# A Nystrom attention and expert-layer kernel whose order of work is laid down anew

## The chip, the cores and the metric

The kernel runs on one core of one Trainium2 chip. The metric is the time of one execution on the device in microseconds (us), as the median of several runs. One more execution was profiled; its trace gives the instructions of every engine: TensorE (PE, its weight loads PEld), VectorE (DVE), ScalarE (ACT), GpSimd (POOL), and SyncE (SP), which issues nearly all DMAs.

## The reference, cut to what matters

```python
# q, k, v: 8 batches, 8 heads, 576 rows, 64 columns; 32 landmarks (means of 18 rows)
A  = sm(q, k_lm);  Bm = sm(q_lm, k_lm);  C = sm(q_lm, k)     # sm: softmax of scale * a @ b.T
Z = Bm.T / (norm1(Bm) * norminf(Bm) + 1e-6)
for _ in range(6):
    Z = 2 * Z - Z @ Bm @ Z
x = A @ Z @ C @ v                  # then reshaped to 4608 tokens of 512
logits = normed(x) @ normed(expert_emb).T / tau              # 8 experts
expert_idx = argmax(logits); gate_w = softmax(logits)[expert_idx]
out[token] = gate_w * (relu(x @ w1[expert_idx]) @ w2[expert_idx])   # w1 512x1024, w2 1024x512
```

## The kernel before, in words

The kernel works batch by batch, and the steps of the eight batches are woven into one another. For a batch b it guesses the one expert that all its tokens choose, loads that expert's weights, and checks the guess at the end (a general path follows when a guess fails).

Steps of a batch, each a Python generator in `nystrom_moe` (L477): `loads` (L638, keys and queries, 1152 KB each; those of batch 0 in two parts), `load_values` (L655, two halves of 640 KB, two buffers), `sums` (L666, the landmarks' means, on POOL and DVE or DVE alone), `guess` and `choose` (L1150, L1171, the expert), `inverse` (L691) and `powers` (L1020, the six steps of the inverse; batches 2 and 3, 4 and 5, 6 and 7 are taken together), `values` (L798, pooled-query scores), `weighted` (L872, the landmarks' values), `queries` (L914, attention scores) with `scored` (L941, their softmax, with `both`, L977, a subtraction or a product on POOL or DVE), `landmarks` (L1069), `rows` (L1192, router scores and norms of the tokens, two steps a batch), `weights` (L1318, four loads of 512 KB for w1 and four for w2), `first_scale` (L1339, each quarter of w1 squared and summed at L1348), `first_weights` (L1369, the landmark products folded into w1), `scaled` (L1401, their split into two 16-bit parts), `second_weights` (L1426, the scale and the split of w2), `first` (L1487, the first layer: six products of 288 columns a chunk), `second` (L1516, the second layer: three products of 512 columns a chunk) and `outputs` (L1556, scaling on ACT or DVE, and the store). All products except transposes and warming are issued through the helper at L514.

Some buffers tie the steps: eight PSUM banks; of these four in a row ("quad") are used by one step at a time among `values`, `queries`, `rows` and `first_weights`; two buffers for keys, queries and values; four each for the quarters of w1 and of w2.

The order of all this is written out by hand in four constants: TURNS (L59), a string of 2614 two-character numbers, each of which names the generator that goes on next; CHOICES, which engine a step takes where there is a choice; BANKS, which PSUM banks a step gets; and WARM, at which turn how many units of 128 columns of warming products are put ahead of a step. `Weave.run` (L222) walks through them, and each engine's instructions, and SP's DMAs, are issued in the order of the walk:

```python
        for turn, n in enumerate(turns):
            ask, got = self.asks[n], None
            if ask[0] == "any":
                option = ask[1][int(next(choices))]
...
            elif ask[1] == "pe":
                if turn in WARM:
                    warm(WARM[turn])
...
                    got = self._banks(int(next(banks)), ask[6])
            self._step(n, got)
```

`keep_warm` (L600) issues the warming products, whose results nobody reads, into the last bank (L604), up to 512 columns each. They stand only in the first part of the program, before the first layer of batch 0.

Of the kernel before, what the change touches and what calls it, by code (L numbers as in the profile page):

```python
# [59 lines left out]
    "0606063306330033000706060700340c0b340b38013801010001010800383e000100083f010h013636013g3g003j3k360c37010101010c"  # L60
    "01360h0136390c0139003j0i013j1i013u3k3u013w3u3x3v3x1j3w3x1j3w3w3x3v1i3x3n3x3u3x3x3k3h3x3x3l3x3x1k3l3x3u3v3x3x3h"
    "3u1m3h1k3u3x3h1i0d3x3x3h3w1k3h3a3u3v3a1i1i1j021k3w0d3a1l411i021k3u02413u410e1l3w1k1k1k1k3u3w3w1k1i3a1k02001k1k"
    "1i0e1l411k3w1k1k3a020n1k1k3u1k413o1k421k1k1k3w1k1j1k3u3m4602421k46421k3m1l1k0n3a2m1j1j1j3w1j3a432m462m49431m49"
    "2m02022m4h3a3m2m2m3m024i3m4h1n3o023w3o3a2m1m02024k4l0i4j4j4m1m4i4m021m2m2m2m4o3a022m2m1m4p4o024p1n2m1n1n1n4q2m"
    "023a1n4r4q1m1m2n4u1n0i021m1m1m1m024p1m2m1m022m0i4u1m2m0o4t4s4v1n4t2m2m4x4z1m4s4x2m1m504z510o4v1m51524w4w2n2m2m"
    "1m4p1o2n1m1m55502n2m1m524w2n3b542n1m1p541o1o1o4r1m2n3b1m4y2n564y1m1m4w3b4w4y563b3p4w3p584w59551p1r0o4y2n2n2n59"
    "2n53584w2n2n4w534w3c583c0o533c3c2n2n4w2n2n1r4r532n592n4w2n3c2n2n1p0t1o4q5c2n1o2n4w3c1o1r4n4n5c585c584w1o591r3d"
    "5c4w033d584w2n2n2n2n591p032n593d035h0j2n4n5h5h4n585h4w4w2n1p2n4n03581p4n031r2n1p58035h5h5h0358035h5h5h5h5b3q03"
    "1r034a2n03591r5b2n1r3q1r035b2n0303033q3q2n033q2n581r1p2n5j03031p3q5g2n5d035k0359595k5l5l5d5k5j5g5k1q2n4b1p5k58"
    "5l581p5n5m3q5l0j592n5m2n592n2n2n1r1r2n595l3q1r5n1r5m595l5n2n1r2n4b5q4b5l2o372o1r2o5d2o5r5l3q5l5p5l5s5s5s5s5s5p"  # L70
    "1r5u5s5u5s3q5l0k5g3q3q5l2o5w1r2o5z5l5w5x5z2o2o2o5w2p5x5l5v5l0k5x5y5v1r2o2o5y1r2o5t5t1r63612p5l0u5t2p2o5t605l1r"
    "605t0p645l64632p611r2o5t4d4d3r4d0u1r663m664d3q3r4d2p3a4d3r5j0t683r2p682o6868683r6g2o4d4d3s6h6g676h6h6h3s3s0z3s"
    "3s2o673t2o5p4d3t3t0p1s1s4d6j6i1t1t2o2o1s2p674c6i1s4c6o6m6j1s6m2p2o6n6o1t366n1t2o6p6p6a2o6q2o6o2p1s6a6r1s6r6q6n"
    "6a6k1t2p2p2p2p2p6n6s0q6k2p1t6t6u6o2p1u6k2p6n6k6o6n6u6n6u2p1u6u0q6n1s4d1w2p0z1t1u6k2p6u2p6u2p6u0u7a6n6n6n0u6k7a"
    "6o6k6n6o6k4d792p7a6k6o6o796o6n1t6k6k2p2p2p2p2p2p2p791u6o7c7c4e2p6o6o7c2p6v4e1u1w6w6v6w1u1w6v4e102p4e2p2p6v2p6v"
    "6v6c6c104f7b6c6c781w6c781w7b2p6c4f4f7f1w1u1u2p691u782p7b2p4f7f1u7f4f1w7f0v2p1w4f152p1w1u1w4a7e7g7f7g7g1v7h6c71"
    "2p1w1w2p1w6c7h7j7e7i2p2p2p7h0v2p3n4g2p7i2p0w4g7i706b6b7n4g7l1w7o7j0w1w1w7l7j107m107l7m2q2q2q2q7j7r1w1y2q7n2q2q"
    "1w1w1w2q7u1x1x7o2q2q1w7v7t7s2q7t1y2q2q1x1x1x1x7o7x7r2q7o7x7e2q2q7z2r7v2q7s807z7w2q2q1y1y7y1x7w7o1z7y2q1w7q8015"
    "7n6c7u7q7n1x1w6c2q1w2q6c2r2r2r1y827q1y1y812q2q6c2r847n81828e7m848d2r2r8c8e7o8d7q1z2r8c2r7n2r717n2r7o717o8i218h"
    "048j2r2r8j041z8j1z7o161z7n7j2r042r211y21041z047o042r2r212r2r8j1z7o047m8j7m8j7m1z7m8g7n8g16048g2r042104047m7m6c"  # L80
    "212r2r2r1z1z8j2r8p2r2r212r2r217m21218q2r2r8o041b1z8p7n04047m7m2r8r8q202r047n048o1b047m8s0404218t8o048p7n914d8s"
# [34 lines left out]
WARM = {20: 36, 39: 6, 42: 2, 51: 13, 63: 19, 77: 4, 86: 10, 93: 21, 104: 24, 123: 19, 157: 9, 188: 19}  # L116
# [1571 lines left out]
```

## Time and profile before

| what | us |
|---|---|
| median of 3 runs | 401.57 (401.19 to 401.67) |
| the profiled execution | 400.33 |
| its span, first to last instruction | 398.6 |
| TensorE busy | 382.6 |
| DVE busy | 319.3 |
| ACT busy | 252.8 |
| POOL busy | 88.0 |

The profiled execution's own time stands beside its span: 1.7 us lie around the span. A profile's "idle before" of an instruction is time in which its engine did nothing, and the name behind the arrow is what ended it; "issue" means that nothing shown there was waited for. The mean granted clock of TensorE over the span is 0.999 of full speed.

### The profile page before, as it was taken

To read this page: it belongs to the slowest core of one execution; us is meant where nothing else is said; L and a number is where in the kernel's file an instruction comes from. 1 tells how busy PE (TensorE), PEld (TensorE's weight loads), DVE (VectorE), ACT (ScalarE), POOL (GpSimd) and SP (SyncE) were. 2 spreads that over 40 slices of the span, in tenths; PEclk is the share of its full clock that TensorE was granted. 3 is DMA by queue.
4 is the path that set the end of the run, shared out by engine and by line. 5 is a ranking of instruction groups with operands and counts; after the bars stand their busy time and mean duration, and the time that the engine had idled before them with its cause. 6 is when DMAs were issued, how large, how long until landed. Compare 5 with 4: busy or idle time off the path is not lost.

```text
span 398.6 us, 15203 instructions
## 1 busy us (share of the span) xinstructions
PE 382.6 (96%) x6390; PEld 237.4 (60%) x6390; DVE 319.3 (80%) x916; ACT 252.8 (63%) x627; POOL 88.0 (22%) x91
## 2 busy tenths in 40 slices
PE   3999999999999999999999999999999999999994
PEld 1456755586645775567754675557745675467644
DVE  5899998899898999977989999747896798747431
ACT  1369969578589779735978678155659749445310
POOL 4154255211203132302335711101101201000100
PEclk9999999999999999999999999999999999999999
DMA  8887973563695996226786776114480266116012
GB/s 305 344 323 321 389 268 124 154 248 118 181 407 212 303 404 226 74 71 236 242 322 244 249 224 216 63 42 152 133 314 12 81 196 242 53 47 233 2 41 88
DMA packets 22669, 78.78 MB, mean 198 GB/s; under 512 B 2752, under 2 KB 5056, under 8 KB 20800
## 3 DMA queue, kind: packets, MB, share of 16 engines
q1 hardware_dynamic: 22304, 77.54, 53.7%
q8 instruction: 52, 0.85, 0.9%
q10 hardware_dynamic: 288, 0.18, 0.2%
q14 instruction: 25, 0.20, 0.2%
HBM read 62.96 MB, written 14.75 MB: 195 GB/s over the span
## 4 chain that ended last, share of the span: by engine, by line
PE 85%; DVE 6%; ACT 5%; issue 1%; DMA 1%; POOL 0%; ACTq 0%; DVEq 0%
PE ps L514 82%; PE ps L604 3%; ACT junk L1232 2%; ACT ec L861 2%; DMA k_t<-kT 1%; DVE ww L1418 1%; DVE w2c L1472 1%; DVE cm L824 1%; DVE ht L1482 1%; ACT ht L1480 0%; DVE cneg L851 0%; POOL half L682 0%; ACT ww L1416 0%; PE ps L1105 0%; ACT w2c L1470 0%
## 5 line engine op out<-in xcount | busy, mean ns | idle before, releaser
L514 PE MATMUL ps<-w2c,ht 128*128 128x512 f16 (+2 forms) x1176 | 197.6, 340 | 0.1
L514 PEld LDWEIGHTS <-ht 128*128 128x128 f16 (+1 forms) x1176 | 94.7, 102 | 80.3 <-issue 1.4
L514 PE MATMUL ps<-ab,ww 128*128 128x288 f16 x768 | 100.7, 286 | 0.8 <-DVE gpr L1167 0.5
L514 PEld LDWEIGHTS <-ww 128*128 128x128 f16 x768 | 73.6, 98 | 23.9 <-issue 2.0
L1480 ACT ACTIVATE ht<-ps 128x288 f16<-128x288 f32 x128 | 47.5, 424 | 26.4 <-PE ps L514 24.8
L1482 DVE SCALAR_TENSOR_TENSOR ht<-ps,ht 128x288 f16<-128x288 f32 x128 | 53.8, 448 | 9.6 <-ACT ht L1480 8.7
L1232 ACT ACTIVATE junk<-ps 128x512 bf16<-128x512 f32 (+1 forms) x40 | 23.8, 596 | 26.2 <-DVE lga L1223 12.3
L1472 DVE SCALAR_TENSOR_TENSOR w2c<-wstage,wsc,w2c 128x1024 f16<-128x1024 f32 x28 | 37.4, 1337 | 3.0 <-ACT w2c L1470 2.8
L1348 ACT ACTIVATE junk<-wstage 128x1024 bf16<-128x1024 f32 x32 | 34.0, 1064 | 6.2 <-DMA wstage<-w 6.0
L1574 ACT ACTIVATE yt<-ps,gfac 128x512 f32<-128x512 f32 (+1 forms) x30 | 18.8, 627 | 22.7 <-PE ps L514 20.7
L861 ACT ACTIVATE ec<-ps,cneg 128x144 f32<-128x144 f32 x64 | 23.4, 390 | 11.0 <-DVE cneg L851 5.6
L1250 POOL TENSOR_TENSOR nrm<-ssq,half 128x5 f32<-128x5 f32 x8 | 10.4, 1300 | 85.6 <-ACT junk L1232 85.6
L981 POOL TENSOR_TENSOR ae<-ae,asum 128x576 f32<-128x576 f32 x11 | 12.7, 1157 | 71.3 <-DVE asum L795 23.3
L1432 ACT ACTIVATE junk<-wstage 128x1024 bf16<-128x1024 f32 x26 | 27.4, 1055 | 1.5 <-DMA wstage<-w 1.3
L1470 ACT ACTIVATE w2c<-wstage,wsc 128x1024 f16<-128x1024 f32 x21 | 24.2, 1159 | 2.8 <-DVE wsc L1443 2.8
L682 POOL TENSOR_TENSOR half<-q_t 128x576 f32<-128x576 f32 x13 | 19.5, 1500 | 28.8 <-DVE ht L1482 11.8
L972 POOL TENSOR_TENSOR ab<-at,ab 128x576 f16<-128x576 f32 x11 | 14.1, 1286 | 48.7 <-ACT ab L970 38.4
L1416 ACT ACTIVATE ww<-ps,wsc 128x1024 f16<-128x1024 f32 (+1 forms) x18 | 17.8, 1023 | 10.4 <-PE ps L514 9.1
L1418 DVE SCALAR_TENSOR_TENSOR ww<-ps,wsc,ww 128x1024 f16<-128x1024 f32 (+1 forms) x18 | 20.7, 1159 | 3.6 <-ACT ww L1416 3.6
L682 POOL TENSOR_TENSOR half<-k_t 128x576 f32<-128x576 f32 x11 | 14.5, 1314 | 21.5 <-DMA k_t<-kT 12.9
L981 POOL TENSOR_TENSOR ae<-ae,am 128x576 f32<-128x576 f32 x11 | 12.7, 1158 | 26.6 <-DVE am L955 25.0
L514 PE MATMUL ps<-wstage,wt 64*32 64x256 f32 x512 | 16.8, 380 | 1.0 <-issue 0.7
(220 smaller groups left out, 505.9 us busy)
## 6 DMA issues: line engine op xcount, KB each, us to landing
wstage<-w SPq DMA_DIRECT2D x64, 512.0 KB, 6.7
v<-v SPq DMA_DIRECT2D x16, 640.0 KB, 5.9
k_t<-kT SPq DMA_DIRECT2D x7, 1152.0 KB, 10.9
q_t<-qT SPq DMA_DIRECT2D x7, 1152.0 KB, 7.2
out<-yt SPq DMA_DIRECT2D x31, 256.0 KB, 2.9
abs__140<-ab SPq DMA_DIRECT2D x8, 576.0 KB, 3.8
k_t<-kT SPq DMA_DIRECT2D x2, 576.0 KB, 4.8
q_t<-qT SPq DMA_DIRECT2D x2, 576.0 KB, 6.7
```

The lines of the kernel that those rows point to most:

```text
L514: pe.matmul(o, lhsT, rhs, start=start, stop=stop)
L682: pool.tensor_tensor(out=half, in0=sv[:, :, :, 0:9], in1=sv[:, :, :, 9:18], op=ALU.add)
L861: act.activation(ects[g][:, QS * x:QS * x + QS], pc[:, a, c], AF.Exp, bias=neg[:, 4 * g + 2 * a + c:4 * g + 2 * a + c + 1], scale=SCALE / ...
L981: pool.tensor_tensor(out=x, in0=x, in1=z, op=op)
L1232: act.activation(junk[lo:hi, 0:512].rearrange("p (j g x) -> p j g x", j=4, g=2), pfv[lo:hi, :, n, :, 0:D], AF.Square, scale=1.0 / ASCALE, ...
L1348: act.activation(junk, stage[1, b, q], AF.Square, accum_out=sq[:, q:q + 1])
L1418: vec.scalar_tensor_tensor(out=ww[:, 1], in0=pw, scalar=sc, in1=ww[:, 0], op0=ALU.mult, op1=ALU.subtract)
L1432: act.activation(junk, stage[2, b, q], AF.Abs, accum_out=sq[:, q:q + 1])
L1470: act.activation(w[:, 0], st, AF.Copy, scale=sc)
L1472: vec.scalar_tensor_tensor(out=w[:, 1], in0=st, scalar=sc, in1=w[:, 0], op0=ALU.mult, op1=ALU.subtract)
L1480: act.activation(ht[:, 0, r], ph[:, 0:HS], AF.Relu)
L1482: vec.scalar_tensor_tensor(out=ht[:, 1, r], in0=ph[:, 0:HS], scalar=0.0, in1=ht[:, 0, r], op0=ALU.max, op1=ALU.subtract)
```

## The change

Only the four constants change. The generators, the instructions they issue, the shapes and the loads are the same. The strings say nothing to a reader, so here is the head of each, and WARM in full:

```diff
 TURNS = (
-    "0606063306330033000706060700340c0b340b38013801010001010800383e000100083f010h013636013g3g003j3k360c37010101010c"
+    "0606063333060b0b0007000033060607083c3c010836013601003600010001340c3f010c003g010c3h01013435013h340c010101340134"
...
 CHOICES = (
-    "01110001100100010000000000000000000100011111010000100000001000110010111100001011001010000000000010010000000000"
+    "01110011000100100000000000000000000100011001010000000000000100100011000011111001100010000000000000100010000000"
...
 BANKS = (
-    "40261016010541230201010107123012703436512370612020162063426325473420340130210456730113421242321413241232703170"
+    "00201616010531230201201107123701273453602371601771604701320341257302040120305467212031423141231423412134014021"
...
-WARM = {20: 36, 39: 6, 42: 2, 51: 13, 63: 19, 77: 4, 86: 10, 93: 21, 104: 24, 123: 19, 157: 9, 188: 19}
+WARM = {19: 36, 31: 5, 49: 13, 78: 16, 87: 15, 103: 21, 117: 21, 142: 12, 157: 9, 188: 7}
```

Walked through turn by turn, the two orders differ in this:

- **Loads at the start (SP).** Before: keys and queries of batch 0, values of batch 0, keys and queries of batch 1, then w2's first quarter, w1's first two, the first half of batch 1's values, w1's third and fourth quarter, the second half of the values, the rest of w2, the keys of batch 2. After: the same to the queries of batch 1, then w1's first two quarters, w2's first, w1's third, both halves of the values, w1's fourth, two quarters of w2, the keys of batch 2, and w2's last quarter.
- **The inverse of batch 0.** After, its first power is issued between the two halves of the attention scores of batch 0, where it came behind both; on DVE some transposes and reductions of the scores stand between the powers that stood ahead of them.
- **`weighted` of batch 4.** Before, `inverse` (4, 5), `first_weights` 3, the first power and `weighted` 4 follow one another; after, three chunks of the second layer (nine products of 512 columns) stand ahead of the first power.
- **The four banks in a row.** Between the two `rows` steps of batch 5: before, two chunks of the second layer and one power; after, five chunks, one chunk of the first layer and two powers. Between the second `rows` step of batch 3 and `queries` of batch 4: after, three chunks of the second layer and one power. Between the two `rows` steps of batch 1: the same chunks in both.
- **Choices.** Output scalings: 30 on ACT and 11 on DVE before, 24 and 17 after. `both`: 22 on POOL and 10 on DVE before, 27 and 5 after. Passes over w2 on DVE where ACT could do them: 13 before, 16 after.
- **Warming.** 182 units of 128 columns before, 155 after; before the first power and before the second half of `queries` 0 none is left.
- **The last stores** stand in the same order.

## Rows read from the trace of the kernel before

**Rows 1.** The page, head and part 1: share of the span.

```profile
span 398.6 us, 15203 instructions
PE 382.6 (96%) x6390; PEld 237.4 (60%) x6390; DVE 319.3 (80%) x916; ACT 252.8 (63%) x627; POOL 88.0 (22%) x91
```

**Rows 2.** The page, part 4: chain that ended last, by line.

```profile
PE ps L514 82%; PE ps L604 3%; ACT junk L1232 2%; ACT ec L861 2%; DMA k_t<-kT 1%; DVE ww L1418 1%; DVE w2c L1472 1%; DVE cm L824 1%; DVE ht L1482 1%; ACT ht L1480 0%; DVE cneg L851 0%; POOL half L682 0%; ACT ww L1416 0%; PE ps L1105 0%; ACT w2c L1470 0%
```

**Rows 3.** Windows: us, PE, PEld, DVE, ACT, POOL busy, clock, DMA share, GB/s.

```profile
0.00:40.30 40.30, 31.45 (x715) 17.92 (x716) 33.14 (x118) 20.29 (x51) 16.80 (x36) 1.00 0.84 322
40.30:393.60 353.30, 351.15 (x5676) 219.48 (x5675) 286.17 (x799) 232.02 (x576) 71.17 (x56) 1.00 0.52 185
393.60:398.60 5.00, 0.02 (x1) 0.00 (x0) 0.00 (x0) 0.47 (x1) 0.00 (x0) 0.96 0.16 51
```

**Rows 4.** Windows within the first 40 us, same columns.

```profile
18.50:26.55 8.05, 8.05 (x219) 4.44 (x204) 8.05 (x21) 3.34 (x6) 4.80 (x4) 1.00 0.83 295
26.55:35.10 8.55, 7.19 (x167) 4.04 (x164) 7.33 (x41) 7.21 (x15) 3.93 (x4) 1.00 1.02 398
35.10:40.30 5.20, 5.11 (x141) 3.80 (x141) 5.17 (x19) 5.20 (x13) 2.12 (x2) 1.00 0.55 211
```

**Rows 5.** Windows for L604 (warming) alone: us, PE, PEld; the sum.

```profile
18.50:26.55 8.05, 4.46 (x19) 1.63 (x20) 1.00 0.83 295
...
sum 28.60, PE 13.78 PEld 4.43; mean PE 3.44 PEld 1.11
```

**Rows 6.** Waits of PE, 40.3 to 394 us: total, times, longest.

```profile
PE ps L514 <- ACT junk L1232: 0.9, 3, 0.4
PE ps L514 <- issue: 0.6, 1, 0.6
```

**Rows 7.** Timeline of PE around 168.9: start, us, what, idle before.

```profile
167.76 0.52 PE L514 MATMUL ps<-v,ct 128*32 128x64 f32 x22
168.91 0.88 PE L514 MATMUL ps<-v,ct 128*32 128x64 f32 x48 [0.64 <-issue]
```

**Rows 8.** DMA queues, 166 to 167.6 us: packets, MB, share.

```profile
q1 hardware_dynamic: 36, 0.07, 12.2%
q8 instruction: 1, 0.02, 5.6%
```

**Rows 9.** DMA queues, 27.8 to 29 us.

```profile
q1 hardware_dynamic: 113, 0.42, 95.5%
q8 instruction: 1, 0.02, 4.9%
```

**Rows 10.** Timeline of PE, first-layer weights of batch 0.

```profile
30.24 0.40 PE L514 MATMUL ps<-wstage,wt 64*32 64x256 f32 x1 [0.68 <-issue]
```

**Rows 11.** Timeline of PE around the rows steps of batch 5.

```profile
263.56 0.57 PE L514 MATMUL ps<-wgd,ab 32*128 32x72 f16 x48
264.06 1.47 PE L514 MATMUL ps<-w2c,ht 128*128 128x512 f16 x6
265.46 0.65 PE L514 MATMUL ps<-ek 32*32 32x64 f32 x32
266.46 0.77 PE L514 MATMUL ps<-wgd,ab 32*128 32x72 f16 x72 [0.36 <-ACT junk L1232]
```

**Rows 12.** Timeline of PE, second rows step of batch 1.

```profile
100.20 0.77 PE L514 MATMUL ps<-wgd,ab 32*128 32x72 f16 x72 [0.41 <-ACT junk L1232]
```

**Rows 13.** Groups by line: output scaling on DVE.

```profile
L1572 DVE TENSOR_SCALAR yt<-ps,gfac 128x512 f32<-128x512 f32 (+1 forms) x11 | 7.8, 715 | 3.9 <-PE ps L514 3.8
```

**Rows 14.** DMA issues, 23.5-24, 24-24.5 and 25.8-26.2: KB, us to landing.

```profile
wstage<-w SPq DMA_DIRECT2D x1, 512.0 KB, 4.7
...
wstage<-w SPq DMA_DIRECT2D x1, 512.0 KB, 6.8
...
v<-v SPq DMA_DIRECT2D x1, 640.0 KB, 6.6
```

**Rows 15.** Timeline of PE: first expert product.

```profile
35.10 0.28 PE L514 MATMUL ps<-ab,ww 128*128 128x288 f16 x1 [0.49 <-DVE gpr L1167]
```

More of the change, by code (lines that the diff above doesn't have):

```diff
@@ L65 @@
[L65 to L69, printed above, removed]
@@ new lines @@
+    "3p3o3n3o3i3n1k1k3i3n3m1m3p3i3o3i3o38380d0e3m3p0e381k0202421k023p421i00421k2n383p3n3n1k1k021k3n1k1l1k1k021k1l1k"
+    "1k421k443s02381j3p1l1k1k023n1i3q1k1k001k1k471k1k0n3p3n3p1k3q1k421j44471j1k441l381k2m3p451j2m38471j493p452m3q1m"
+    "02022m4a3q492m2m022m3q4b0i3s4a4c4d0i3s1j2m024f4b1m2m4c4e1m384g2m2m1m2m4g4i022m0i0n4l4m1m024i02024e022m1m1m1m02"
+    "021m4k2m4e2m024l2n1m4j1m1n2m2m4x4w1m4u1m4y4k2m4w1m1m4x2m4j4w1m1n4u4y2m1m2m2m2m1m1n1m4e3838521n0i1n1m2n4z4v0o50"
+    "1n0o504z1o4v2n2n551o1m51511m522n381m391m1m534w54394w392n2n394w0t1o4w551r1m1p3t533t1o55582n542n2n584m591o2n2n2n"
@@ new lines @@
+    "4w55590o3a0o1r4w4w562n2n2n2n564w2n3a564l3a563a2n1o4m2n2n5b3a3a582n3b2n1r5b4w2n3b1o583b5b2n354w4h4h4w595d5b1n1p"
+    "035d1o1p4w4n4w4h4w5858031r5d031r2n2n1r2n2n5d4h58035d031n032n2n4h03032n0j591p5d584h592n4w3u1r5d5d0j0303035d034o"
+    "031p03591p033u5d3u2n5d5a591p3u035a582n3u590k033u5c2n5k58031r5859035k5k1p1r5g5k5c032n5k1p0k592n5a2n5g591p1p5n58"
+    "2n5l591q5o5n5l3u2n2n5p5o1r1r5n1r1r2n2n5l5p593u2n2n585o1r5p1r2n2n2n5l4o5q4o2p5l1r5l5r5l5l2o5s5t1r5g5q5l2o5v2o5w"
+    "5t2o5t5t5t5l5t5t5l5x5l2o2o5x5y1r3u343u5x2o2o2o1r5w2o602o0t612o0u601r0u3u635v625y5y1r5l5u5u5l5l5z6b3u5l3u5z5l1r"
@@ new lines @@
+    "635u625u2p6c1r5l0p5u2o2p5c615u6b2o1r6e4q2p4q3v6e4q3v4q4q4q3v3v3v2p6f2p6c6f2o6f6f6f4q0p644q2o653w6i6i5q6g6g3w2o"
+    "2o3w6i6i2o3w2o2p3w4q4q1t6k3x4p6j6c3x6k6j1t4p3x1t4q6n6o0u6m6l6n1t2o6p1t0q1s6o6o6m386n2o6n1w2o2p1s0u1t6q6l1s1s0z"
+    "656m652o6p2p6q6w6t1w6w6s6m6u2p2p1t6u2p1s2p6n2p2p2p6o6u6u6u6u6o6m6o6u6z6n0z6o6o6o6o2p2p1s2p1u6o1t4q2p6z6m6n6y2p"
+    "6m2p782p153q6m0q6m6y1s6m6n6z6n2p6r1s6m2p2p6y2p2p6x2p2p6x2p2p6n6m7a2p6n6m104r6v1u7a1w6r4r6v6v6v6v6v1u2p2p676n2p"
+    "1u1u1w781w6n4r671u4r4s67671w4s4s6r674s1u1u1u1u7a2p672p2p7e2p107g1w1u7e2p0v4s1w7e4s1w1w1v7e7e7g67784t0v7h7h151w"
@@ new lines @@
+    "7i677i7f1w2p2p1w2p7h2p2p2p2p2p2p7i662r7t0w2q0w1w7r3r4t667f7f1w7v717t2q7r7r7s7s7w4t7v1w2q2q2q7r101y101w7w2q2q2q"
+    "1y1w1w1w1w2q81827x2q817y2q831x7z1x1x1w847g2q1x1x4q842r1x1x2q2q2q2q7y2q6x7z861w7v85807t7x862r1y2q888783871y7x2q"
+    "2q2q7v1z828980807v2q1w852q2r2q2r881y218b7t898d7x8d7x1x1y8e7x2r2r8b8e808a718a7t717x042r2r6721042r2r7t8f1z1y1z1z"
+    "7t8g042r7t8h1y8h212r2r21677x2r6i7t21672r8h1z2r8h1z7r8h21047v2r1z041z04048h218h161z2r2r7v2r2r2r2r2r677v7x8n7x04"
+    "4n8o047x212r1z2r0404161z21207v8p0404047s8n2r042r8o8j672r8p2r8n7t21217v8o2121047v048j048t218r7t04048s8u8u8u2r7t"
@@ new lines @@
+    "8i8i7v8r8u2r8r8u8i8t70118u2r2r117t8s7v8u8i8u8s8i692s8u21698u8i8u8u2s2s8w2r21698q2r2s692s8w698u8u68212r8q682r68"
+    "7l8u2r8u68211b688y728u8y8x6a8u737273902r902r2r2r6a926a738x2r2r90732r2r738p92902r732r8z949394948z94941b93907l93"
+    "1673738j9e93217l219f95952s169d9g8z2s2s9i9e9e9g129e9g9i9g9g2s731c2t9g1c229g2s9k9l22222s93222s9k229l2192222s2s2s"
+    "2s1290239n23929p9o232s9s222s9p73229r9r90932s239s2s9q2s902124932s2t232s2t939w909q2t2t2t8t9u9w909v9o24217k95929n"
+    "9n2t8q909x9z9u2s249va173239o21909x9h9z9h7m23927ma31c2t9ha4929324a123a32t9ha32t93929h90262473732t1c2t2ta42t9h7n"
```

72 lines of the change are left out of this document (26 added, 46 removed).

## The prediction

> **What bounds the kernel now.** I read the page's head first, for the span and TensorE's share [rows 1], then the chain that ended last [rows 2]. TensorE's products at L514 are 82% of the chain, with the other engines at a few per cent. Then I cut the span into three stages [rows 3]. From 40.3 to 393.6 us TensorE is busy 351.15 of 353.30 us, so it stands idle for 2.15 us of that stage, while VectorE (DVE) is idle for 67 us. The last 5 us are the last scaling and its store. The first 40.3 us are another matter: TensorE is busy for 31.45 us there, of which 13.78 us are the warming products at L604 [rows 5], so it does 17.7 us of useful work and 22.6 us are spent on waiting.
>
> What limits that first stage is read from three windows in it [rows 4]. DVE is busy 8.05 of 8.05 us from 18.5 to 26.55 and the DMA engines are at 1.02 of their share from 26.55 to 35.1. The start is thus a chain of vector operations beside a full load queue, and TensorE waits for both.
>
> The change lays down the order anew and adds or removes no product but warming ones. So it can gain in three places only: the 22.6 us at the start, the 2.15 us of idle time in the body, and nothing at the end, since the order of the last stores is the same in both.
>
> **The body, wait by wait.** TensorE's waits after 40.3 us are few [rows 6]: 0.6 us in one piece put down to "issue" and 0.9 us in three for the squares at L1232 (a trifle more for L861).
>
> The "issue" piece is at 168.91, between two products of one landmark-value step, where TensorE waits for no other engine [rows 7]. Just before it, the program queue q8 moved one packet: 5.6% of 16 engines over 1.6 us, which is 1.43 us in one engine [rows 8]. I read the stall as TensorE running out of fetched instructions, in a stretch of many short products. In the old order this step (batch 4, L872) comes after a product of `inverse` (L691), a first-layer weight step (L1369) and one power of the inverse (L1020), with no expert product between. The new order puts nine products of 512 columns in there. Six of those take 1.47 us [rows 11], so nine take 2.2 us, with only 18 instructions, and the fetch can catch up. **Term: -0.64 us.** Bounds: -0.64 (gone) and +0.64 (there, and once more elsewhere).
>
> Is it true that a fetch waits for loads, which is what the new replay assumes? One fetch stands in a full queue, another in a nearly empty one. From 27.8 to 29.0, with loads at 95.5%, the packet took 4.9% of 16 engines over 1.2 us, 0.94 us [rows 9]. From 166.0 to 167.6, with loads at 12.2%, it took 1.43 us [rows 8]. Load traffic did not make the packet longer; what it waited before it started, no row shows. So of the two rules in the replay I count on the distance, not on the waiting. The Trainium skill bears on this (DMA: Bandwidth & Descriptors, section "Queues, rings and completion order"): each DMA engine goes round robin between the queue rows with work, a packet at a time, so that a fetch on its own row would not stand behind all loads of another. These two packets agree with that. By that rule the waiting rule of the replay would move steps for nothing, and the sum would lack this term if the waiting alone were to bring it.
>
> The waits for the squares: the rows steps (L1192), the attention scores, the pooled queries and the first-layer weight steps share one set of four PSUM banks, so each waits until its predecessor's scores are reduced and squared. At 266.46 TensorE waited 0.36 us for this [rows 11]: between the two rows steps of batch 5 stood six products of 512 columns and one inverse step (ek), from 264.06 to 266.1. The new order has fifteen such products, six of 288 columns and two inverse steps there, over 5 us. That wait goes. **Term: -0.36 us.** The wait at 100.20 (0.41 us) [rows 12] stays, since both orders put the same chunks between the two rows steps of batch 1. New narrow places: between the second rows step of batch 3 and the scores of batch 4 stand nine products of 512 columns (2.2 us) and an inverse step, fewer than in the old order. At batch 5 the release took from 264.13, the end of the first rows step, to 266.46, so 2.3 us. So this is either no wait or one like that at 100.20: 0 to +0.41, and I take the middle. **Term: +0.2 us.**
>
> **The start.** The expert products begin at 35.10 [rows 15]. They need all four quarters of the first expert's w1 squared. In the old order SP issues a quarter of w2, two quarters of w1, the values of batch 1 (first half, which must wait for a buffer), w1's third and fourth quarter, and then the second half of the values. The fourth quarter was issued within 24 to 24.5 us and took 6.8 us [rows 14], so it landed at about 31. The new order issues w1's first two quarters before w2's, the third before the values, but the fourth after both halves of the values. The second half waits for the landmark-value step that frees its buffer, and left at 25.8 to 26.2 [rows 14]. So the fourth quarter leaves at about 26.4, behind one value load. The third quarter of the old order, also behind one value load alone, took 4.7 us [rows 14]: 26.4 + 4.7 = 31.1, where it was 31. **Term: 0.** Bounds: with the 6.8 us of the old fourth quarter it lands at 33.2, +2.2 us; and below, the 0.68 us stall at 30.24 [rows 10] may go, -0.68. I take 0, for the row of one value load ahead is the nearest case.
>
> On DVE, which is full there, the order of single operations changes, but what has to be done before the inverse ends is the same set but for a few reciprocals. I put it at nothing, within the bounds above.
>
> **Warming and choice of engine.** Warming falls from 182 units of 128 columns to 155. At 13.78 us for all [rows 5] that is some 2 us of busy time less, at a place where TensorE waits for DVE and loads: 0, covered by these waits. The choices move work: six more output scalings on DVE (6 x 715 ns = 4.3 us [rows 13]), five fewer of the 128x576 subtractions and products there (these go to POOL), three more passes over w2 on DVE instead of ScalarE. The cover is DVE's 67 idle us in the body [rows 3], so 0; where DVE is full for 10 us on end, some of it could show, and that is in the range.
>
> **Sum:** 0 - 0.64 - 0.36 + 0.2 = -0.8 us. The profiled execution took 400.33 us (its span 398.6 and 1.7 around it), 1.24 under the median of 401.57; against the median the forecast is 400.8. A measurement of this kernel can tell about 0.2%, 0.8 us, from no change, so this sits on the edge between faster and the same.
>
> **Rivals.** *A longer start (slower).* The fourth quarter of w1 lands late, since the second value load, and the step that frees its buffer, now stand ahead of it. It decides from a landing past about 31.5: each us of that moves the whole expert part. At 33.2 the time is 400.8 + 2.2 = 403.0. For it: the full queue [rows 4]. Against: 4.7 us is the nearer row. 0.19.
>
> *A shorter start.* The two first quarters of w1 come one load earlier, the third waits for no buffer, and the stall at 30.24 [rows 10] goes with its cluster: 400.8 - 0.7 = 400.1, and with some DVE time filled 399.5. 0.22.
>
> *The stalls only move* (the change doesn't do what it says). Other stretches of short products in the new order are as dense, so fetch stalls or bank waits of 0.4 to 0.7 us come in their place: 400.8 + 1.0 = 401.8, from 401.2 to 402.5. 0.18.
>
> *The clock falls.* With fewer warming products, and none between the first transposed product and the second step of the inverse, TensorE could drop. The granted clock was 1.00 (2.4 GHz) in all windows of the start [rows 4]. From 18.5 to 26.55 TensorE was busy all 8.05 us, 4.46 of them with warming [rows 5]: at 1.2 GHz the other 3.6 us would take twice that, at most +3.6, 404.4. Against: the gaps that lose their warming hold other products. 0.03. The Trainium skill has this rule (TensorE: Matmul & The Clock Gate, "Part 1: The HAM clock gate"): how busy the array has been decides between the two clocks, and idle is the slow one. By it fewer fillers are a risk; the rows here show no drop to weigh it by.
>
> **How the numbers follow.** Forecast 0.38, with a range of its own of 399.9 to 401.6: half of it faster by over 0.2%, half the same. The shorter start is all faster; the moved stalls 0.11 the same, 0.04 slower, 0.03 faster; the longer start and the clock 0.21 slower, 0.01 the same. Together faster 0.44, same 0.31, slower 0.25. The range leaves out the far end of the longer start and of the shorter one: 398.9 to 403.4.
>
> **What would show it.** Right: no idle piece by "issue" of over 0.5 us in the body; no wait for L1232 between the rows steps of batch 5; idle time of TensorE after its first expert product at or under 1.5 us; that first product within 0.5 us of 35.1; granted clock 1.00. Wrong: a first expert product past 36, with ScalarE's pass at L1348 waiting for the w1 load, would be the longer start; one before 34.3 the shorter; as much idle time in the body as before, at other steps, the moved stalls.

## The result, and the profile after

The changed kernel takes 404.5 us (median of 20 runs, 402.01 to 407.42), the kernel before 401.54 us in the same comparisons (20 runs, 400.25 to 404.66). The ratio is 1.0066, with a 95% interval of 1.0048 to 1.0085: slower by some 0.7%, 2.7 us (3.0 us by the two medians). The ratios in this document are taken over the runs of one comparison, leave out the two slow ones among them (both of the kernel before), and are not the quotients of the medians beside them. The forecast was 400.8 us with a range to 403.4.

The profiled execution of the changed kernel took 402.01 us, which is the fastest of its 20 runs. So its trace shows only a part of the loss, and the rest has to be looked for in other executions (below). The page's head and its first part, then three windows (columns as in [rows 3]):

```profile
span 400.3 us, 15184 instructions
PE 381.4 (95%) x6383; PEld 236.3 (59%) x6383; DVE 320.2 (80%) x917; ACT 248.5 (62%) x622; POOL 93.4 (23%) x96
```

```profile
0.00:40.30 40.30, 30.44 (x713) 17.42 (x714) 33.58 (x116) 19.53 (x48) 16.95 (x36) 1.00 0.86 324
40.30:393.60 353.30, 350.93 (x5673) 218.90 (x5670) 285.91 (x800) 228.86 (x575) 76.40 (x60) 1.00 0.51 185
393.60:400.30 6.70, 0.00 (x0) 0.00 (x0) 0.75 (x1) 0.08 (x1) 0.00 (x0) 0.63 0.21 70
```

The body is as full as before [rows 3]. The third window is not: TensorE is done, as before, but the span goes on for 6.7 us where it went on for 5.0, and DVE has an instruction there that it did not have.

Some of TensorE's waits over the whole span (total, times, longest):

```profile
PE ps L514 <- DVE ws L1003: 1.5, 3, 1.0
...
PE ps L514 <- DVE cm L824: 0.7, 1, 0.7
PE ps L514 <- DVE ht L1482: 0.6, 2, 0.3
...
PE ps L514 <- ACT junk L1232: 0.5, 2, 0.3
PE ps L514 <- DVE ww L1418: 0.4, 1, 0.4
```

There is no wait by "issue", and those for L1232 fell from 0.9 us to 0.5 [rows 6]. TensorE around its first expert product, which starts at 33.90 where it started at 35.10 [rows 15]:

```profile
32.92 0.16 PE L514 MATMUL ps<-ws,ones 128*128 128x1 bf16 x1 [1.04 <-DVE ws L1003]
33.90 0.42 PE L514 MATMUL ps<-ab,ww 128*128 128x288 f16 x2
34.74 0.66 PE L514 MATMUL ps<-ab,ww 128*128 128x288 f16 x4 [0.42 <-DVE ww L1418]
...
41.59 0.65 PE L514 MATMUL ps<-ab,ww 128*128 128x288 f16 x4 [0.30 <-DVE ht L1482]
```

So the start is 1.2 us shorter at the first product; 0.42 us go at 34.74, and by 43 us the lead is gone (0.30 us of it at 41.59), since ScalarE waited until 39.48 for w2's last quarter, which now stands behind batch 2's keys. **In this execution the last scaling on ScalarE, right behind TensorE's last products, starts 0.45 us earlier than before (393.20, not 393.65), and the span is 1.7 us longer.** The loss lies in the last 20 us. First the timeline of the kernel before, all engines:

```profile
381.33 0.16 DVE L1610 CAST mis<-misf 128x1 bf16<-128x1 f32 x1
382.32 0.34 SPq L1579 DMA_DIRECT2D out<-yt  x1
...
386.89 0.17 PE L514 MATMUL ps<-mis,ones 128*128 128x1 bf16 x1
...
387.98 0.34 SPq L1579 DMA_DIRECT2D out<-yt  x1
...
391.09 1.14 DVE L1572 TENSOR_SCALAR yt<-ps,gfac 128x256 f32<-128x256 f32 x2 [3.81 <-PE ps L514]
393.65 0.47 ACT L1574 ACTIVATE yt<-ps,gfac 128x256 f32<-128x256 f32 x1 [9.76 <-PE ps L514]
394.16 0.36 ACTq L1579 DMA_DIRECT2D out<-yt  x1
```

and of the changed kernel:

```profile
380.62 0.16 DVE L1610 CAST mis<-misf 128x1 bf16<-128x1 f32 x1
...
382.81 0.69 ACT L1574 ACTIVATE yt<-ps,gfac 128x512 f32<-128x512 f32 x1 [3.99 <-issue]
390.03 0.17 PE L514 MATMUL ps<-mis,ones 128*128 128x1 bf16 x1
390.06 3.11 PE L514 MATMUL ps<-w2c,ht 128*128 128x256 f16 x27
390.26 0.16 DVE L1614 CAST misi<-ps 128x1 int32<-128x1 f32 x1 [9.05 <-PE ps L514]
391.12 4.04 SPq L1579 DMA_DIRECT2D out<-yt  x3
391.17 0.48 DVE L1572 TENSOR_SCALAR yt<-ps,gfac 128x256 f32<-128x256 f32 x1 [0.74 <-PE ps L514]
393.20 0.47 ACT L1574 ACTIVATE yt<-ps,gfac 128x256 f32<-128x256 f32 x1 [9.71 <-PE ps L514]
393.71 0.36 ACTq L1579 DMA_DIRECT2D out<-yt  x1
394.05 0.75 DVE L1572 TENSOR_SCALAR yt<-ps,gfac 128x512 f32<-128x512 f32 x1 [2.39 <-DMA out<-yt]
```

The product that adds up the wrong guesses (`mistakes`, `ps<-mis,ones`) had its input at 380.8 us and was issued at 390.03, ahead of the last 27 products, where before it stood at 386.89, ahead of the last 54. SP reads its result in `outputs` (L1562, a register load) before it may issue the next store, and the stores behind that read on SP's queue wait with it. SP's wait at that read, in the kernel before and in the changed one:

```profile
SPq L1562 <- DVE misi L1614: 4.6, 1, 4.6
...
SPq L1562 <- DVE misi L1614: 7.5, 1, 7.5
```

The chunk that ScalarE scaled at 382.81 leaves at 391.12 (before, the one scaled at 383.21 leaves at 387.98, behind the same read). `outputs` has three `yt` buffers. The last full chunk's scaling on DVE finds none free and waits 2.39 us for that store, which the chain of work that ended last shows ahead of it:

```profile
391.12 2.84 DMA out<-yt
```

Its own store is the last thing in the program. After the last scaling on ScalarE starts, the span goes on for 400.3 - 393.20 = 7.1 us, where it was 398.6 - 393.65 = 4.95 us: **2.1 us are lost behind TensorE's end.**

### The profile page after: what moved, and what is told of

Same layout as the page of the kernel before. It is cut to its first block, busy times and chain, and to the rows that moved or that the text cites. A ratio compares the mean times of both kernels' runs of the same rounds, so it can differ in the third digit from the quotient of the medians.

```text
span 400.3 us, 15184 instructions
## 1 busy us (share of the span) xinstructions
PE 381.4 (95%) x6383; PEld 236.3 (59%) x6383; DVE 320.2 (80%) x917; ACT 248.5 (62%) x622; POOL 93.4 (23%) x96
## 4 chain that ended last, share of the span: by engine, by line
PE 74%; DVE 12%; DMA 5%; ACT 3%; issue 3%; POOL 0%; SPq 0%; DVEq 0%; ACTq 0%
PE ps L514 73%; DMA wstage<-w 4%; DVE ht L1482 2%; ACT ec L861 1%; DVE cm L824 1%; DMA k_t<-kT 1%; ACT junk L1232 1%; DVE w2c L1472 1%; DVE qsum L685 1%; DMA out<-yt 1%; DVE ww L1418 1%; DVE ek L1035 1%; ACT ht L1480 1%; DVE asum L961 0%; PE ps L1105 0%
## 5 line engine op out<-in xcount | busy, mean ns | idle before, releaser
L1480 ACT ACTIVATE ht<-ps 128x288 f16<-128x288 f32 x128 | 46.5, 418 | 25.7 <-PE ps L514 25.6
L1232 ACT ACTIVATE junk<-ps 128x512 bf16<-128x512 f32 (+1 forms) x40 | 23.9, 597 | 30.5 <-DVE lga L1223 20.8
L1472 DVE SCALAR_TENSOR_TENSOR w2c<-wstage,wsc,w2c 128x1024 f16<-128x1024 f32 x28 | 35.6, 1275 | 0.4 <-ACT w2c L1470 0.2
L1348 ACT ACTIVATE junk<-wstage 128x1024 bf16<-128x1024 f32 x32 | 33.9, 1060 | 2.6 <-DMA wstage<-w 2.2
L1250 POOL TENSOR_TENSOR nrm<-ssq,half 128x5 f32<-128x5 f32 x8 | 9.4, 1177 | 105.6 <-ACT junk L1232 105.4
L861 ACT ACTIVATE ec<-ps,cneg 128x144 f32<-128x144 f32 x64 | 23.5, 390 | 12.3 <-DVE cneg L851 7.6
L1432 ACT ACTIVATE junk<-wstage 128x1024 bf16<-128x1024 f32 x25 | 26.4, 1056 | 4.2 <-DMA wstage<-w 3.9
L981 POOL TENSOR_TENSOR ae<-ae,asum 128x576 f32<-128x576 f32 x13 | 15.1, 1169 | 39.9 <-DVE asum L795 21.5
L1574 ACT ACTIVATE yt<-ps,gfac 128x512 f32<-128x512 f32 (+1 forms) x24 | 15.0, 642 | 13.7 <-PE ps L514 9.7
L1470 ACT ACTIVATE w2c<-wstage,wsc 128x1024 f16<-128x1024 f32 x19 | 21.7, 1155 | 0.0
L981 POOL TENSOR_TENSOR ae<-ae,am 128x576 f32<-128x576 f32 x14 | 16.2, 1161 | 21.8 <-DVE am L955 13.6
L682 POOL TENSOR_TENSOR half<-k_t 128x576 f32<-128x576 f32 x11 | 14.3, 1297 | 25.6 <-DMA k_t<-kT 13.2
L514 PE MATMUL ps<-ek 32*32 32x64 f32 (+1 forms) x768 | 16.0, 214 | 0.8 <-DVE ek L1035 0.7
```

The source lines that it names most:

```text
L514: pe.matmul(o, lhsT, rhs, start=start, stop=stop)
L682: pool.tensor_tensor(out=half, in0=sv[:, :, :, 0:9], in1=sv[:, :, :, 9:18], op=ALU.add)
L861: act.activation(ects[g][:, QS * x:QS * x + QS], pc[:, a, c], AF.Exp, bias=neg[:, 4 * g + 2 * a + c:4 * g + 2 * a + c + 1], scale=SCALE / ...
L981: pool.tensor_tensor(out=x, in0=x, in1=z, op=op)
L1232: act.activation(junk[lo:hi, 0:512].rearrange("p (j g x) -> p j g x", j=4, g=2), pfv[lo:hi, :, n, :, 0:D], AF.Square, scale=1.0 / ASCALE, ...
L1348: act.activation(junk, stage[1, b, q], AF.Square, accum_out=sq[:, q:q + 1])
```

## The experiments

Most edits move turns in the four strings (one changes a line of `outputs`, one a number in WARM); the walks below have one line a turn, in words, since the strings say nothing to a reader. Medians stand beside that of the kernel before on the same chip.

**First question: is it the place of the check?** Theory: it costs the 2.1 us, by SP's queue and the `yt` buffers. Rival: the loss comes from the start or the body, and the tail only follows. Four kernels ran on one chip (before: 401.0 us, 35 runs).

*The check early*, in the changed kernel:

```diff
+mistakes: the last DVE steps, the sum on TensorE (bank 1, now 0)
 second b=7 c=2 f=6
...
-mistakes: the last DVE steps, the sum on TensorE
 second b=7 c=3 f=7, first half
```

> The changed kernel with the check product of `mistakes` put back to where the old order had it (ahead of the sixth part of the second layer's third chunk of batch 7). Theory TAIL (the late check holds SP, the held store holds a yt buffer, and the last scaling on DVE waits for that store): the DVE scaling that waited until 394.05 runs right behind its products, the span falls by about 2.1 us to 398.2 in the profile, and the ratio to the kernel before falls from 1.0066 to about 1.001. Rival START (the loss lies in the first 45 us, loads in a worse order, and the tail is only where the profile ends): ratio stays at 1.005 or more.

*A buffer of its own*: the check stays late, but the last full chunk is scaled into a buffer that nothing else uses then.

```diff
-        yt = wst.tile([P, DM], F32, name="yt", bufs=BUFS["yt"])
+        if (b, c) == (B - 1, 2):
+            yt = wst.tile([P, 1024], F32, tag="st1", name="wstage", bufs=BUFS["st1"])
+        else:
+            yt = wst.tile([P, DM], F32, name="yt", bufs=BUFS["yt"])
```

> The changed kernel, check still late, but the very last scaled chunk (chunk 2 of batch 7) is written to a free weight staging buffer and not to one of the three yt buffers. TAIL: the last DVE scaling no longer waits for a store, the stores still leave SP late; most of the 2.1 us comes back, ratio 1.001 to 1.003. If SP alone (late stores, not the buffer) made the tail: no gain, 1.006. START: 1.006.

*The kernel before with the check late*, that one turn moved and one bank renumbered:

```diff
-mistakes: the sum on TensorE
 second b=7 c=2 f=6
...
+mistakes: the sum on TensorE
 second b=7 c=3 f=7, first half
```

> The kernel before with only its check product put late, where the new order has it (ahead of the last part of the second layer's chunk 3 first half). TAIL: it gets slower by about 2 us, ratio 1.004 to 1.006, with a DVE scaling of L1572 that waits for an out store. START: ratio 1.000.

*The changed kernel again*, with no edit:

> The changed kernel unchanged, for a second profile beside the first and for the same chip as the others. TAIL: ratio 1.006 to 1.007, last scaling waits for the store again by 2 us or more. The profile also tells what lies between this kernel's profiled 402.0 us and its median of 404.5: START expects late loads in the first 45 us (first quarter squares at L1348 waiting over 1.5 us), a clock theory expects a granted clock under 1.00 in the first 40 us.

| kernel | us, median | ratio to before, 95% interval | last scaling on ScalarE to the end of the span, us |
|---|---|---|---|
| changed, check early | 402.59 (12 runs) | 1.0014 (0.9982 to 1.0047) | 401.8 - 396.43 = 5.4 |
| changed, own buffer | 403.31 (10) | 1.0037 (1.0000 to 1.0074) | 399.6 - 394.37 = 5.2 |
| before, check late | 404.16 (10) | 1.0061 (1.0025 to 1.0096) | 401.2 - 394.13 = 7.1 |
| changed, again | 405.15 (10) | 1.0077 (1.0038 to 1.0115) | 403.4 - 396.37 = 7.0 |

The last column settles it for the tail: 7.0 to 7.1 us with the check late in either order, 5.0 to 5.4 us with it early or with a buffer of its own. In the kernel before with the check late, DVE waits as in the changed one:

```profile
390.96 0.17 PE L514 MATMUL ps<-mis,ones 128*128 128x1 bf16 x1
...
394.96 0.75 DVE L1572 TENSOR_SCALAR yt<-ps,gfac 128x512 f32<-128x512 f32 x1 [2.09 <-DMA out<-yt]
```

So one turn moved down by 27 products costs 0.6% (0.25 to 0.96), and the way it does so goes through the buffer: giving the waiting chunk another buffer takes the two microseconds of the tail away while the check stays late. That is shown by the last column; the times alone would not tell it, since the 1.0037 with the own buffer is above the 1.001 to 1.003 that was expected, and its interval overlaps that of the repeat.

**Second question: what else?** With the check early the ratio came out as expected (1.0014), but the span did not (401.8 us, not 398.2). The kernel has won back 2.6 us against its own repeat, but nothing of the 0.8 us that was forecast is there, and in the repeat's profiled run (405.15 us) the last scaling on ScalarE starts 3.2 us later than in the first profile (396.37, not 393.20). The repeat's start, as TensorE's timeline:

```profile
34.64 0.16 PE L514 MATMUL ps<-ws,ones 128*128 128x1 bf16 x1 [2.59 <-DVE ws L1003]
...
35.76 1.84 PE L514 MATMUL ps<-ab,ww 128*128 128x288 f16 x6
```

and a window behind that wait (the clock is the column behind POOL's):

```profile
34.90:38.30 3.40, 3.36 (x46) 1.70 (x33) 3.36 (x14) 3.40 (x8) 1.27 (x1) 0.50 0.84 352
```

The first expert product starts at 35.76, not 33.90, and then the granted clock is 0.50, the lower of the two levels (1.2 GHz), for 3.4 us: six products take 1.84 us. The run with the check early shows the same after a wait of 1.83 us, with 3.4 us at 0.50:

```profile
33.76 0.16 PE L514 MATMUL ps<-ws,ones 128*128 128x1 bf16 x1 [1.83 <-DVE ws L1003]
...
34.96 1.77 PE L514 MATMUL ps<-ab,ww 128*128 128x288 f16 x6
```

```profile
33.90:37.30 3.40, 3.40 (x46) 1.86 (x46) 3.36 (x13) 3.40 (x7) 1.28 (x1) 0.50 0.97 404
```

What TensorE waits for is ScalarE's pass at L1348 over w1's fourth quarter, and that pass waits for the load. It started at 31.53 us in the first profile of the changed kernel, and at 32.33, 32.37 and 33.25 in the three others with that order of loads; in the kernel before it started at 30.96 and waited for no load.

A second place is at 341 us, where TensorE needs the sums over batch 7's weights. The repeat waits 1.36 us there, and so does the run with the check early, whose lines these are:

```profile
341.55 0.16 PE L514 MATMUL ps<-ws,ones 128*128 128x1 bf16 x1 [0.45 <-DVE ws L1003]
...
344.40 0.16 PE L514 MATMUL ps<-ws,ones 128*128 128x1 bf16 x1 [1.36 <-DVE ws L1003]
```

Batch 7's loads, too, are in another order than before: w2's quarters go ahead of w1's, and on ScalarE the passes over w1's last two quarters stand behind the pass over w2's last, which waits for its load.

Theory: these two are the rest of the loss. Rivals: the waits are covered; or the clock falls for want of warming. Four kernels ran on a second chip (before: 400.91 us, 35 runs).

*The start*, on top of the check early:

```diff
 load_values b=1, first half
+weights b=0 w1, fourth quarter
 load_values b=1, second half
...
-weights b=0 w1, fourth quarter
...
+weights b=0 w2, fourth quarter
 loads b=2, keys
-weights b=0 w2, fourth quarter
```

> The changed kernel with the check early, and two loads of the start moved on SP's queue: the fourth quarter of w1 of batch 0 ahead of the second value load of batch 1, and the last quarter of w2 of batch 0 ahead of the keys of batch 2. Theory (the late quarter of w1 costs the start, and the clock falls when TensorE waits long enough for it): ScalarE's wait for wstage ahead of L1348 falls from 1.9 us to under 0.7 us, TensorE's wait for ws (L1003) between 31 and 35 us from 1.8 us to under 0.7 us, no stretch at a granted clock of 0.5 between 30 and 40 us, and the time against before goes from 1.0014 to 0.997 to 1.000. Rival (the start's loss is not the load): the waits go and the time stays within 1.000 to 1.003, the values of batch 1 being late in its place.

*The start and batch 7*, on top of that:

```diff
+weights b=7 w1, third and fourth quarter
 weights b=7 w2, third quarter
...
+first_scale b=7, passes over the third and fourth quarter (ScalarE)
 second_weights b=7, pass over the fourth quarter (ScalarE)
...
+first_scale b=7, sum and scale
 second b=6 c=1 f=6
...
-second_weights b=7, sum and scale; first_scale b=7, sum and scale
...
+second_weights b=7, sum and scale
 second b=6 c=2 f=5
```

> The same, and batch 7's loads in another order: all four quarters of w1 ahead of the third of w2, their passes on ScalarE ahead of that over the last quarter of w2, and the sum over w2 on TensorE behind the next chunk's products. Theory (1.5 to 2.1 us are lost near 341 us since the sum over w1 waits behind the last quarter of w2): TensorE's waits for ws (L1003) after 300 us fall from 1.8 us to under 0.3 us, and the time is 0.3 to 0.5% under the run with the start alone: 0.993 to 0.997 of before. Rival (the first layer of batch 7 waits in their place, or TensorE's later waits take it back): the waits near 341 us go, others of 1 us or more come up to 365 us, and the time stays within 0.1% of the run with the start alone.

*More warming*, on top of the check early, loads as they were:

```diff
-WARM = {19: 36, 31: 5, 49: 13, 78: 16, 87: 15, 103: 21, 117: 21, 142: 12, 157: 9, 188: 7}
+WARM = {19: 36, 31: 5, 49: 13, 78: 16, 87: 15, 103: 21, 117: 21, 142: 12, 157: 9, 188: 31}
```

> The changed kernel with the check early, loads as they were, and 31 units of 128 columns of warming in place of 7 ahead of the sum over the last quarter of w1 of batch 0 (1.3 us more of it in the gap from 31.9 us on). Theory (the clock falls because TensorE is idle for 1.8 us or more while it waits for that quarter): the wait for the load on ScalarE stays at 1 to 3 us, but no stretch at a granted clock of 0.5 follows; in runs where it would have fallen some 1.5 to 2 us are saved, so 0.997 to 1.000 of before where it was 1.0014. Rival (the clock falls for another reason, or its fall costs little): a stretch at 0.5 of some 3.4 us is still there, or the time is 1.000 to 1.003.

*The kernel before with the quarter late*:

```diff
-weights b=0 w1, fourth quarter
 load_values b=1, second half
+weights b=0 w1, fourth quarter
```

> The kernel before, with one load moved on SP's queue: the fourth quarter of w1 of batch 0 behind the second value load of batch 1. Theory (this place is what made the start long): the quarter lands past 32 us, ScalarE waits 1 us or more ahead of L1348, the first expert product starts at 36 to 37.5 us in place of 35.1, and the time is 1.003 to 1.008 of before. Rival (the step of the prediction held: behind one value load it lands at 31.1 as before): first expert product within 0.4 us of 35.1, time 0.999 to 1.001.

| kernel | us, median (12 runs each) | ratio to before, 95% interval |
|---|---|---|
| check early, start | 400.42 | 0.9987 (0.9974 to 1.0001) |
| check early, start, batch 7 | 400.55 | 0.9974 (0.9952 to 0.9995) |
| check early, more warming | 402.16 | 1.0038 (1.0006 to 1.0069) |
| before, quarter late | 402.37 | 1.0039 (1.0013 to 1.0064) |

The start is confirmed from both sides, though the edit that mends it moves two loads at once, and how much each of them brought is not shown. With w1's quarter ahead of the second value load, ScalarE waits for it no more, TensorE does not wait for the sum, and the clock stays:

```profile
32.88 0.16 PE L514 MATMUL ps<-ws,ones 128*128 128x1 bf16 x1
...
33.87 0.42 PE L514 MATMUL ps<-ab,ww 128*128 128x288 f16 x2
```

```profile
33.90:37.30 3.40, 2.97 (x56) 1.99 (x55) 3.40 (x13) 3.40 (x9) 1.28 (x1) 1.00 0.72 299
```

In the kernel before, that one load moved behind the other gives it what the changed kernel had, the lower clock included, though its first expert product, at 35.42, is hardly late: the expectation of 36 us fell, that of the time held. Twelve products take 2.52 us, where twelve at 35.31 in the run with the start mended take 1.63 us:

```profile
35.42 2.52 PE L514 MATMUL ps<-ab,ww 128*128 128x288 f16 x12 [0.67 <-DVE gpr L1167]
```

```profile
36.00:39.00 3.00, 3.00 (x18) 1.89 (x17) 2.71 (x13) 2.55 (x6) 0.28 (x1) 0.50 0.54 222
```

The Trainium skill tells of this (TensorE: Matmul & The Clock Gate, "HAM oscillation — how this bites in real kernels"): a wait for a transfer can set the array back to its slow clock, so that the work behind the wait is paid at half speed. The two windows at 0.50 behind waits of 1.8 and 2.6 us agree. The last one, behind no wait of TensorE over 0.7 us, is not of that kind.

More warming kept the clock at 1.00 in the profiled run (the load was waited for 1.4 us there), but the time did not come down: 1.0038, and the expectation of 0.997 to 1.000 fell. Every run also carries its mean granted clock over the span. It is under 0.996 in 8 of the 12 runs with the check early (on the first chip), and on the second in 1 of 12 with more warming and in none of 12 with the start mended (the kernel before: 8 of 34 and 4 of 34 on these two chips). So the warming did keep the clock, and the kernel was still 1.7 us slower by the medians than with the loads moved, on the same chip. Filling the gap with warming doesn't replace the load: the work behind the gap still starts late.

The profiles show it too. The run with more warming, at 1.00, starts its first expert product at the time of the run with the check early, at 0.50 (34.93 and 34.96), and comes to the second rows step of batch 1 no sooner. First its lines, then that of the run with the check early:

```profile
34.93 0.42 PE L514 MATMUL ps<-ab,ww 128*128 128x288 f16 x2
...
101.42 0.77 PE L514 MATMUL ps<-wgd,ab 32*128 32x72 f16 x72 [0.17 <-ACT junk L1232]
```

```profile
101.05 0.77 PE L514 MATMUL ps<-wgd,ab 32*128 32x72 f16 x72 [0.17 <-ACT junk L1232]
```

From the first expert product to that step it is 65.5 to 65.6 us in the four profiles with the start's loads moved. With the loads late it is 66.1 and 66.3 us where the clock fell, and 65.6, 66.3 and 66.5 us where it stayed; in the last two of these TensorE waited for `ht` near 42 us (0.30 and 0.42 us), with w2's last quarter late on ScalarE. So in this order the late loads cost the later first product and up to 1.0 us behind it, and what the lower clock costs by itself is not shown. In the kernel before with the quarter late it is clearer: the first product comes 0.3 us later than in the profile of before, that step 1.8 us later (102.03, not 100.20), so 1.5 us go behind the first product in this execution, where the clock is at 0.50.

Batch 7's loads did less than was expected. The waits at 341 us went (1.2 us in the profile with the start alone, 1.8 us in that with the check early), but 0.9 us came back a little later, as the rival had it:

```profile
353.82 0.57 PE L514 MATMUL ps<-wgd,ab 32*128 32x72 f16 x48 [0.90 <-DVE ww L1418]
```

With the sum over w2 moved behind a chunk, DVE did two pairs of passes over w2 (4 us) ahead of the first-layer weights for which the rows step's banks wait. Whether a gain in time is left is not shown: the median is that of the start alone, the ratio a little lower (0.9974, not 0.9987), with intervals that overlap.

**Third question: do the parts add up, and was the fetch stall the order's?** Three kernels ran on a third chip (before: 400.69 us, 23 runs).

*The first-layer weights ahead*, on top of all the above:

```diff
+scaled b=7, both halves (L1418 on DVE)
 second_weights b=7, first two quarters (L1468, L1472 on DVE)
...
-scaled b=7, both halves (L1418 on DVE)
```

> The kernel with the check early, the start's loads and batch 7's loads moved, and on DVE the first-layer weights of batch 7 (L1418) ahead of two passes over w2 (L1468, L1472). Theory (the 0.9 us wait for ww at 353.8 us in the run without this came from those passes, 4 us of DVE work ahead of it): that wait falls to under 0.3 us, TensorE's last product ends some 0.9 us earlier against before than in that run, and the time is 0.994 to 0.998 of before. Rival (a wait of the same size comes later, or the gain is lost in the last store): TensorE's waits after 345 us stay at 0.9 us or more, and the time is 0.997 to 1.000.

*The start alone*: the changed kernel with the edit of the start, the check left late.

> The changed kernel, with the two loads of the start moved and nothing else: the check stays late. Theory (the check and the start are separate losses that add up, 0.5 to 0.6% for the check and 0.3% for the start): 1.003 to 1.006 of before, where the changed kernel was 1.0066 and 1.0077; no stretch at a granted clock of 0.5; the last scaling on DVE (L1572) still waits 2 to 2.5 us for out<-yt. Rival (the start alone is the loss, and the check matters only with it): 0.998 to 1.002. Other rival (the start matters only once the check is early): 1.0065 or more.

*The kernel before, again*, with no edit:

> The kernel before, unchanged. The stall of 0.64 us by issue at 168.91 us, which the prediction took out of the sum, was not there in the two runs that had the old order at that place. Theory (a fetch stall belongs to one execution, not to the order): no wait by issue of over 0.3 us within 1 us of the same product; one elsewhere, or none. Rival (it belongs to the order): 0.4 to 0.8 us by issue between 167 and 171 us.

| kernel | us, median | ratio to before, 95% interval |
|---|---|---|
| all four edits | 399.34 (12 runs) | 0.9973 (0.9950 to 0.9995) |
| start alone | 401.52 (12 runs) | 1.0008 (0.9983 to 1.0033) |
| before, again | 400.07 (one run, profiled) | |

With all four edits there is no wait of TensorE left after 300 us, and the kernel is 1.35 us faster than before by the medians. It beats both kernels: its 12 runs lie within 398.8 to 400.7 us, the 23 of before within 399.0 to 404.7. What the last edit brought is seen in that wait alone: the ratio without it was the same (0.9974, on the second chip).

The start alone gained more than was expected (1.0008, not 1.003 to 1.006), and came out where a rival had put it: that the start alone is the loss and the check matters only with it (0.998 to 1.002). Against this rival stands the kernel before with the check late, whose start is the old one and which lost 0.6%. Against before, by the medians, the late check and the late start together are +4.15 us (405.15 - 401.0), with the check early +1.6, with the start mended +0.8, with both -0.5. So the start is worth 2.1 to 3.3 us and the check 1.3 to 2.6 us (by the ratios 1.1 to 2.8 and 0.8 to 2.5 us). With intervals of up to 0.4% (1.5 us) to either side the times neither show a plain sum nor speak against it. The tail was there as foretold: DVE's last scaling waits 2.02 us, in this execution put down to ScalarE (`ACT yt L1574`), and the span ends 6.8 us behind ScalarE's last scaling.

And the fetch stall, which the prediction counted at 0.64 us, is not there in the same kernel a second time:

```profile
166.94 0.65 PE L514 MATMUL ps<-ek 32*32 32x64 f32 x32
167.52 0.24 PE L514 MATMUL ps<-cs,ident 128*32 128x2 f32 x8
167.60 1.70 PE L514 MATMUL ps<-v,ct 128*32 128x64 f32 x80
169.23 0.65 PE L514 MATMUL ps<-ek 32*32 32x64 f32 x32
```

The 80 products run through [rows 7]. Of four profiles with the old order in the body, one has the stall there; two have pieces of about 0.2 us, at 273 and 275 us, and one has none. Of nine profiles with the new order one has a stall in the body too, that of the check early:

```profile
127.70 0.43 PE L514 MATMUL ps<-wgd,ab 32*128 32x72 f16 x30 [0.36 <-issue]
```

The other wait by "issue" of the kernel before, 0.68 us at 30.24 [rows 10], does go with the order. It stands ahead of the same product in all four profiles of the old order (0.68, 0.42, 0.34 and 0.22 us) and in none of the nine of the new one. Here is that of the kernel before, again:

```profile
29.98 0.40 PE L514 MATMUL ps<-wstage,wt 64*32 64x256 f32 x1 [0.42 <-issue]
```

## Why the prediction was wrong

**The tail: "nothing at the end, since the order of the last stores is the same in both".** This step failed. The stores stand in the same order, but SP's read of the check stands among them, and the product it waits for had moved 27 products down, from 54 before the last to 27. The forecast followed the queue's order and not what its entries wait for. It cost 2.1 us, shown from both sides. The step's own input is ready at 380.8 us, and nothing but its place holds it for 9 us.

**The start: "4.7 us is the nearer row".** The longer start was named, with its place (the fourth quarter behind both value loads) and a price of 2.2 us, at a chance of 0.19. The load left SP a little earlier than thought (25.3 to 25.6 us, not 26.4), but took 6.2 to 7.8 us from there to its pass, not 4.7, so it landed at 31.5 to 33.3 and past the 31.5 from which it was said to decide. The old fourth quarter's 6.8 us [rows 14], kept as the bound, was the nearer row. By the medians the term that was put at 0 came to 2.1 to 3.3 us, for both late loads of the start (1.1 to 2.8 by the ratios); w1's quarter alone, moved in the kernel before, cost 0.4% (0.1 to 0.6). The fall of the clock had a chance of 0.03, for want of warming, and no place in the longer start. It came in two of the four profiles of this order without more warming, behind the wait for that quarter, and more warming did keep the clock, but it did not give the time back.

**The sign in the profile.** "First product within 0.5 us of 35.1" and "past 36 with L1348 waiting" were meant to tell the cases apart. In the first profile the product came at 33.90, which by the text was the shorter start, and L1348 waited for w1 at the same time. Both were true: other parts of the start are shorter, and the load eats this or more, by execution. Nor is 35.1 firm: the old order's first product came at 34.31 and 34.84 in two more profiles. One profile was not enough to see it.

**Batch 7's loads** were not in the prediction at all. The list of what differs stopped at the start's loads. At 341 us they cost next to nothing in the first profile, and 1.2 to 1.8 us in the three others with that order and no other edit of the loads or the warming.

**The fetch stall: -0.64.** It went, as said, but it was one execution's, not the order's. Against the median, the term is near 0. The stall at 30.24, which the sum kept as a lower bound (-0.68), was the one that the order took away. The reading of the trace as a fetch stall (short products, a packet on q8) fits that execution and was not tested; the step from one execution to the order failed. No run bears on the replay and its two rules, of which the prediction speaks.

**The rows waits: -0.36 and +0.2.** The first was right: the wait at 266.46 is gone. The second was right in size by luck: ahead of batch 4's scores, where it was put, TensorE does not wait for L1232, but one wait of 0.32 us stands in another place, ahead of a first-layer weight step at 129.93. At 100.18, where the wait was to stay, there remain 0.17 us of 0.41.

**Choices and warming: 0.** DVE's busy time in the body is that of before within 0.3 us. New there are three waits of TensorE for DVE, of 0.19 and 0.23 us near 159 us and of 0.32 us near 192 us, which all nine profiles of the new order have; whether a choice of engine brought them was not tested.

## What to carry to other kernels

When an order is changed, list for every in-order queue what each of its entries waits for, and when that now comes: a read of one number on the store queue holds every store behind it until that number's producer is done, however early the producer's inputs are. A load on which the first long products hang goes ahead of loads that aren't due, and warming put into the gap does not replace that. And a stall that shows in one profiled execution is a term of the sum only after a second execution has it too.

## What the runs showed of the hardware

Waits of 1.0 and 1.6 us of TensorE in the gap at 32 us left the granted clock at 1.00; behind waits of 1.8 and 2.6 us it was at 0.50, the lower level, for 3.4 us. In the kernel before with the quarter late it was at 0.50 from 36.0 to 39.0 us with no wait over 0.7 us from 30 us on, so the length of one wait does not tell whether it falls. A lower clock comes in the kernel before without any edit, too: of its 91 runs that count in the ratios of the experiments, 14 have a mean granted clock under 0.996 and took 402.7 to 405.3 us. None of them was profiled, and where the clock fell in them stays open.

The same load, in the same place of the same queue, was in use at 31.5 to 33.3 us from one execution to the next. With it moved ahead and the check early 12 runs lie within 2.5 us (399.0 to 401.5), where the changed kernel's spread over 5.4 us (402.0 to 407.4). Waits by "issue" of 0.2 to 0.6 us of TensorE, read here as fetch stalls, come at changing places, in the same program too; only that at 30.24 us of the kernel before came at its place in every profile of that order, at 0.22 to 0.68 us.
